# Twelve transposes of an identity between the first two score groups, and one key turn moved ahead of the second maxima

## Chip, cores and metric

The kernel runs on one core of a Trainium2 chip. The metric is the device time of one execution in microseconds (us); the figure for a kernel is the median of its runs. Everything is float32.

## The reference, cut to what matters

```
# q, k, v: (8 batches, 8 heads, 576 positions, 64); tau = 0.02
scores = q @ k^T / 8
thresh = max(scores, last axis) - tau
scores = where(scores >= thresh, scores, -1e9)
attn   = softmax(scores)
x      = (attn @ v), heads side by side: 4608 tokens x 512
h = x @ w_in        # 512 x 2048
g = relu(h) ** 2
out = g @ w_out     # 2048 x 512
```

## The kernel before, in words

**Visits and steps.** Attention is done in visits. A visit is one pair of heads of one batch; within a visit the 576 query rows are taken in blocks of 128, with a rest of 64. One block of one visit is a step, numbered s. The first four visits take only their blocks 0 and 1 (steps 0 to 7), so that the first tokens are complete early; later visits take what is left. Step 0 and step 1 are the two blocks of the first visit (number 0), steps 2 and 3 those of the second visit (number 1).

**What a step does, and on which engine.**

- `scores(s)` (line 273): TensorE multiplies 128 queries by the 576 keys, for two heads (u = 0 and 1) and two halves of the keys. That is four products, eight instructions, into two pairs of PSUM banks. Every step uses the first two pairs, banks 0 to 3, except step 1, which uses the list `second`, banks 4 to 7.
- `maxima(s, ...)` (line 310), called at the end of `scores`: VectorE takes the row maxima, one reduction for each head.
- `exponents` (lines 322, 323, 325): ScalarE makes the bias and the threshold from the maxima, and then two exponentials.
- `threshold` (lines 337, 339, 340): VectorE zeroes what is under the threshold, one instruction for each head. These are the last reads of the score banks, so that the next `scores` into the same banks waits for them.
- `divide` (lines 345, 347): GpSimd scales the weights.
- `turn` (lines 386, 387): TensorE transposes the weights by products with an identity, in three parts of three transposes; ScalarE copies each part out of PSUM. In the program of step s the first two parts belong to step s - 2 and stand between `scores(s)` and `exponents` of step s, both on TensorE's queue and on ScalarE's.
- `mix` (line 502): TensorE multiplies turned weights by values, three steps after the scores.

**Keys and queries of a visit.** `load_qk(n)` fetches the rows of visit n, and `prep(n)` turns them with one VectorE instruction each: `prep_part(q, n)` into `qT`, of which there is one buffer, and `prep_part(k, n)` into `kT[n % 2]`, of which there are two (both line 247). `qT` is read by the scores of both steps of a visit, so the queries of visit 1 can be turned only after `scores(1)` has read `qT`. The keys of visit 1 go into the other buffer.

**Start of the program.** After `load_qk(0)`, `load_qk(1)`, `load_v(0)` and the first three weight loads, VectorE does `prep(0)` and scales `ntau8` (line 1005). TensorE does `keep_busy(20)` (line 317): twenty transposes of the identity into bank 7 (`second[1][:, 1, ...]`), whose results nobody reads. Then the loop over s starts.

**What sets the order.** The kernel is scheduled by hand: the order of calls in the program is the order on each engine's queue, and engines wait for each other only by semaphores. In step 0 the loop calls `scores(0)`, `exponents` of step 0, and then, in the block `if s == 0` that the change touches, `scores(1)` and `prep(1)`; then `threshold` of step 0. Step 1 skips its own `scores` for that reason. From step 2 on, GpSimd, VectorE and ScalarE also round the feed-forward weights piece by piece (lines 149 to 158), and SyncE's queue loads keys, queries, values and weights in the order of the program.

From about a twentieth of the span on, the products of the feed-forward part (lines 548, 659, 730, 765) fill TensorE's queue between the score groups.

Of the kernel before, what the change touches and what calls it, by code (L numbers as in the profile page):

```python
# [19 lines left out]
def kernel(  # L20
# [117 lines left out]
    def round_weights(i, stage):  # L138

        words = weight_area(i).bitcast(U32).rearrange("p (n w) -> p n w", w=2)
        lo, hi = words[:, :, 0], words[:, :, 1]
        t, e, d = (turned[:, (i % 3 * 3 + x) * WP:(i % 3 * 3 + x + 1) * WP] for x in range(3))
        tu, eu = t.bitcast(U32), e.bitcast(U32)
        if stage == 0:
            nc.scalar.activation(out=e, in_=hi.bitcast(FP32), func=AF.Prelu, scale=2.0 ** -112, alpha=-2.0 ** 32)
            nc.scalar.activation(out=d, in_=lo, func=AF.Copy, scale=2.0 ** -52)  # L150
        elif stage == 1:
            nc.vector.tensor_scalar(out=tu, in0=eu, scalar1=3, scalar2=None, op0=ALU.logical_shift_left)
        elif stage == 2:
            nc.vector.tensor_scalar(out=eu, in0=tu, scalar1=0xFF800000, scalar2=None, op0=ALU.bitwise_and)
        elif stage == 3:
            nc.gpsimd.tensor_tensor(out=d, in0=d, in1=e, op=ALU.mult)
        else:
            nc.gpsimd.tensor_tensor(out=weight_piece(i)[1], in0=t.rearrange("p (h d) -> p h d", h=2),
                                    in1=d.rearrange("p (h d) -> p h d", h=2), op=ALU.add)

    def rows_of(n):
        return rows_in[n % 2 if n <= 2 * HP else 0]
# [8 lines left out]
    def load_qk(n):  # L171


        for x, t in ((rows_of(n)[1], k), (rows_of(n)[0], q)):
            for m in range(4):
                src, to = rows_32(t, n, m), x[m * 32:(m + 1) * 32, :, :]
                queue = nc.scalar if n == 0 and m % 2 else nc.sync
                last = REST // 32 if t is k and m >= 2 and not by_dma(n) else 0
                queue.dma_start(out=to[:, last:, :], in_=src[:, 0:S // 32 - last, :])
                if last:  # L180
                    queue = nc.gpsimd if n == 0 else nc.sync
                    queue.dma_start(out=to[:, 0:last, :], in_=src[:, S // 32 - last:, :])
# [20 lines left out]
    def arrived(t):  # L203
        assert all(x[0].tensor.name != t.tensor.name for x in loads)
# [27 lines left out]
    def prep(n):  # L232

        prep_part(q, n)
        prep_part(k, n)
# [8 lines left out]
    def prep_part(t, n):  # L244
        to, rows = (qT, rows_of(n)[0]) if t is q else (kT[n % 2], rows_of(n)[1])
        arrived(rows)
        nc.vector.transpose(to, rows.rearrange("p c d -> p (c d)"))
# [10 lines left out]
    def scores(s):  # L258


        vis, i = steps[s]
        n = 2 if i < NBLK else 1
        sc = [(second if s == 1 else pairs)[u] for u in range(n)]
        if i == NBLK:
            for half in range(2):
                nc.tensor.matmul(sc[0][:, half, 0:HALF], qmid, kT[vis % 2][:, half * HALF:(half + 1) * HALF], start=True, stop=True)  # L266
        else:
            halves = [(half, u) for half in range(2) for u in range(n)]
            if early():
                halves.sort(key=lambda x: x[1])  # L270
            for half, u in halves:
                rows = slice(u * D, (u + 1) * D)
                nc.tensor.matmul(sc[u][:, half, 0:HALF], qT[rows, i * P:(i + 1) * P],  # L273
                                 kT[vis % 2][rows, half * HALF:(half + 1) * HALF], start=True, stop=True)
        maxima(s, [x[:, :, 0:HALF] for x in sc])
# [28 lines left out]
    def maxima(s, sc):  # L304
        vis, i = steps[s]
        n = len(sc)
        st = stats[s % len(stats)]
        mx = st[:, 0, 0:n]
        for u in range(n):
            nc.vector.tensor_reduce(out=mx[:, u:u + 1], in_=sc[u], axis=AX.XY, op=ALU.max)  # L310
        w = w_slots[(s - first_dma) % (2 if by_dma(vis) else 3)][:, 0:n, :]
        weights[vis, i] = w, sc, st

    def keep_busy(times):

        for x in range(times):
            nc.tensor.transpose(second[1][:, 1, x % 4 * P:x % 4 * P + P], ident, ident)
# [301 lines left out]
    def some_later(engine):  # L619
        if later[engine]:  # L620
            make(*later[engine].popleft())
# [204 lines left out]
    def by_dma(n):  # L826

        return n >= 3 * HP - 1
# [34 lines left out]
    def early():  # L863
        return state["step"] < min(chunk_at)
# [231 lines left out]
    for s in range(END + 1):  # L1096
        state["step"] = s
        if s >= first_late:
            assert 4 not in kept.values()
            late_step(s)  # L1100
            continue
        state["usable"] = rounded_by[-1]
        rounded_by.append(state["rounded"])
        on = s < NST
        now = []
        if on:
            n, i = steps[s]
            at = visits[n][1].index(i)
            last = at == len(visits[n][1]) - 1
            now = list(range(done, done + pieces[s]))  # L1110
            done += pieces[s]
            more = n + 1 < len(visits)
            short = n < 2 * HP
            if short and at == 0 and 0 < n + 1 < 2 * HP:
                load_qk(n + 2)
            elif not short and at == 1 and not by_dma(n):
                load_qk(n + 1)
            if now:
                round_weights(now[0], 0)
            if s != 1:  # L1120
                scores(s)
                after()
                some_later("gpsimd")
        old = steps[s - 2] if 2 <= s < NST + 2 and not by_dma(steps[s - 2][0]) else None
        at_once = now or old or early()
        lay = on and last and more and not by_dma(n) and s != 1
        if old:
            turn(*old, 0)
            turn(*old, 1)
        if on:  # L1130
            exponents(n, i)
            if s and by_dma(steps[s - 1][0]):
                turn_last(s)
            for p in now[1:]:
                round_weights(p, 0)
            if at == 1:
                split_left(n)
            if lay:
                prep(n + 1)
            elif now:  # L1140
                for p in now:
                    round_weights(p, 1)
        if s in mixes and not old:
            mix(*mixes[s])
            for j in chunk_at.get(s, ()):
                add_chunk(j)
        quarter = rate(s) / 4 if s < END else 1e9
        fill(quarter)
        if s in mixes and old:
            mix(*mixes[s])  # L1150
            for j in chunk_at.get(s, ()):
                add_chunk(j)
        if old:
            turn(*old, 2)
        state["free"] = s > first_dma
        if s == 0:
            scores(1)
            prep(1)
        smooth = s > first_dma + 2 and s not in mixes
        some_later("vector")  # L1160
        some_later("gpsimd")
        if smooth:
            after()
        if on:
            threshold(n, i)
            for fn in prep_at[s] + load_at[s]:
                fn()
            if lay and now:
                round_weights(now[0], 1)
            if now:  # L1170
                round_weights(now[0], 2)
                round_weights(now[0], 3)
            for p in now[1:]:
                assert not lay
                round_weights(p, 2)
                round_weights(p, 3)
            if not at_once:
                divide(n, i)
        if smooth:
            fill(quarter)  # L1180
            after()
            some_later("gpsimd")
        for what in place_at[s]:
            place_blocks(*what)
        some_loads()
        some_later("vector")
        if not smooth:
            some_later("gpsimd")
            fill(quarter)
        some_loads()  # L1190
        if on and at_once:
            divide(n, i)
        fill(quarter)
        some_loads()
        fill(quarter)
        some_loads()
        if on:
            for p in now:
                end_rounding(p)
            if at == 0 and 0 < n <= 2 * HP:  # L1200
                load_v(n)
            elif last and n >= 2 * HP and not by_dma(n):
                load_v(n + 1)
# [35 lines left out]
```

## Time and profile before

| | |
|---|---|
| median of 3 runs | 1334.75 us (1334.66 to 1335.83) |
| profiled execution, its own time | 1334.19 us |
| span of its instructions | 1332.4 us |
| mean granted TensorE clock | 0.995 |
| TensorE busy | 1297.2 us, 97% of the span |
| VectorE busy | 928.2 us, 70% |
| ScalarE busy | 585.2 us, 44% |
| GpSimd busy | 758.3 us, 57% |
| chain that ended last | TensorE 85%, VectorE 5%, ScalarE 4%, DMA 3% |

The profiled execution is 1.8 us longer than its span: what lies before the first and after the last instruction. Its own time is 0.56 us under the median of the runs. Times in the trace count from the start of the span. "PE" is TensorE's matmul, "PEld" its weight load, "DVE" VectorE, "ACT" ScalarE, "POOL" GpSimd, "SP" SyncE. The granted clock is the share of its full clock at which TensorE was allowed to run.

### The profile page before, as it was taken

How to read it: one execution, taken by the hardware profiler on the slowest of the kernel's cores; microseconds unless marked ns; L12 is line 12 of the kernel's file. 1: busy time of each engine (PE TensorE's matmuls, PEld its weight loads, DVE VectorE, ACT ScalarE, POOL GpSimd, SP SyncE). 2: the span in 40 equal slices, each digit the busy share in tenths (PEclk: the TensorE clock that was granted, in tenths of full speed). 3: DMA queues.
4: the chain of work that ended last, by engine and by line, in shares of the span. 5: the costliest groups of instructions: out<-in, count | busy, mean ns of one | idle time of the engine just before them, and what ended most of it. 6: DMA issues, size and time to landing. Idle time of an engine off the chain costs nothing.

```text
span 1332.4 us, 25133 instructions
## 1 busy us (share of the span) xinstructions
PE 1297.2 (97%) x9112; PEld 1078.2 (81%) x9112; DVE 928.2 (70%) x2026; ACT 585.2 (44%) x1357; POOL 758.3 (57%) x865
## 2 busy tenths in 40 slices
PE   7898999999999999999999999999999999999998
PEld 5676556878796979787888888888887888889997
DVE  6877776777787878777786777868687877732131
ACT  4776674235262535343434443444434343422321
POOL 4689875765655555364655554737274737354451
PEclk7999999999999999999999999999999999999999
DMA  8764531647767686867586685758677577430000
GB/s 159 160 152 117 144 91 36 160 93 183 167 177 170 169 195 165 200 141 200 123 186 147 172 192 138 189 108 205 138 181 169 150 180 164 141 91 1 17 17 16
DMA packets 330124, 186.68 MB, mean 140 GB/s; under 512 B 291440, under 2 KB 291472, under 8 KB 323600
## 3 DMA queue, kind: packets, MB, share of 16 engines
q1 hardware_dynamic: 317696, 116.87, 45.0%
q10 hardware_dynamic: 9504, 59.27, 11.2%
q0 software_dynamic: 2800, 8.93, 1.8%
q8 instruction: 72, 1.18, 0.4%
q14 instruction: 52, 0.43, 0.1%
HBM read 109.22 MB, written 68.42 MB: 133 GB/s over the span
## 4 chain that ended last, share of the span: by engine, by line
PE 85%; DVE 5%; ACT 4%; DMA 3%; POOL 2%; issue 1%; SPq 1%; ACTq 0%; DVEq 0%; POOLq 0%
PE big L659 28%; PE big L765 27%; PE big L502 10%; PE big L289 8%; PE big L548 3%; PE big L273 3%; PE big L730 2%; PE big L386 2%; DMA wT<-aside 2%; DVE st L310 1%; DVE w L337 1%; ACT w L325 1%; ACT wT L387 1%; DMA aside<-turned 1%; PE big L266 0%
## 5 line engine op out<-in xcount | busy, mean ns | idle before, releaser
L337 DVE SCALAR_TENSOR_TENSOR w<-big,st,w 128x576 f32<-128x576 f32 x269 | 207.2, 807 | 97.8 <-ACT w L325 97.5
L310 DVE TENSOR_REDUCE st<-big 128x1 f32<-128x576 f32 x288 | 204.3, 748 | 86.2 <-PE big L289 53.5
L347 POOL TENSOR_SCALAR w<-w,st 128x576 f32<-128x576 f32 x269 | 247.4, 929 | 28.0 <-DVE st L340 24.0
L765 PE MATMUL big<-wo,gsum 128*128 128x256 f32 x1088 | 243.8, 382 | 0.0
L345 POOL TENSOR_SCALAR st<-st 128x2 f32<-128x2 f32 (+1 forms) x148 | 36.6, 247 | 358.6 <-DVE w L337 354.2
L765 PEld LDWEIGHTS big<-wo,gsum 128*128 128x128 f32 x1088 | 204.4, 190 | 37.1 <-issue 8.6
L659 PE MATMUL big<-xT,w_in_sb 128*128 128x128 f32 x1536 | 187.3, 277 | 0.8 <-DVE g L671 0.7
L659 PEld LDWEIGHTS big<-xT,w_in_sb 128*128 128x128 f32 x1536 | 178.5, 192 | 9.8 <-issue 7.6
L765 PE MATMUL big<-wo,g 128*128 128x256 f32 x816 | 185.3, 382 | 0.1
L325 ACT ACTIVATE w<-big,st 128x576 f32<-128x576 f32 x269 | 183.8, 734 | 0.2 <-ACT st L323 0.2
L502 PE MATMUL big<-wT,vs 128*64 128x128 f32 (+5 forms) x1700 | 164.8, 355 | 9.7 <-ACT wT L387 4.2
L765 PEld LDWEIGHTS big<-wo,g 128*128 128x128 f32 x816 | 151.6, 190 | 26.1 <-issue 6.5
L502 PEld LDWEIGHTS big<-wT,vs 128*64 128x64 f32 (+1 forms) x1700 | 97.3, 137 | 73.9 <-issue 21.5
L322 ACT ACTIVATE st<-st 128x2 f32<-128x2 f32 (+1 forms) x148 | 30.3, 205 | 263.4 <-DVE st L310 262.2
L671 DVE TENSOR_TENSOR g<-big,g 128x512 f32<-128x512 f32 x96 | 64.8, 677 | 82.3 <-PE big L659 76.4
L289 PE MATMUL big<-kT,qT 64*128 64x320 f32 (+3 forms) x768 | 108.0, 416 | 0.2 <-DVE w L337 0.2
L289 PEld LDWEIGHTS big<-kT,qT 64*128 64x128 f32 x768 | 84.5, 186 | 15.7 <-issue 4.3
L538 POOL TENSOR_TENSOR gsum<-g 128x512 f32<-128x512 f32 x34 | 46.1, 1356 | 81.6 <-ACT g L668 72.1
L667 ACT ACTIVATE g<-g 128x512 f32<-128x512 f32 x96 | 60.3, 628 | 61.0 <-DVE g L671 59.4
L668 ACT ACTIVATE g<-g 128x512 f32<-128x512 f32 x128 | 80.7, 630 | 4.1
L431 DVE STREAM_TRANSPOSE turned<-w 128x512 f32<-128x512 f32 x100 | 70.3, 703 | 3.7 <-DMA aside<-turned 2.6
L437 DVE STREAM_TRANSPOSE turned<-w 128x512 f32<-128x512 f32 x100 | 66.9, 669 | 0.0
(113 smaller groups left out, 1973.2 us busy)
## 6 DMA issues: line engine op xcount, KB each, us to landing
aside<-turned ACTq DMA_DIRECT2D x50, 1152.0 KB, 5.2
wT<-aside SPq DMA_DIRECT2D x200, 288.0 KB, 5.5
vs<-in_v_dram SPq DMA_DIRECT2D x72, 128.0 KB, 4.4
ql<-in_q_dram SPq DMA_DIRECT2D x126, 72.0 KB, 2.9
wo<-in_moe_w_in_dram SPq DMA_DIRECT2D x16, 512.0 KB, 4.8
wo<-in_moe_w_out_dram SPq DMA_DIRECT2D x16, 512.0 KB, 3.7
out_dram<-osb POOLq DMA_DIRECT2D x32, 256.0 KB, 3.3
kl<-in_k_dram SPq DMA_DIRECT2D x113, 72.0 KB, 3.0
```

Source lines behind the costliest of these rows:

```text
L289: nc.tensor.matmul(big[to, at + x0:at + x1], lhsT, keys[u * D:(u + 1) * D, x0:x1], start=True, stop=True)
L310: nc.vector.tensor_reduce(out=mx[:, u:u + 1], in_=sc[u], axis=AX.XY, op=ALU.max)
L325: nc.scalar.activation(out=w[:, u, :].rearrange("p (h k) -> p h k", h=2), in_=sc[u], func=AF.Exp, bias=bias[:, u:u + 1], scale=SCALE)
L337: nc.vector.scalar_tensor_tensor(out=wu, in0=sc[u], scalar=thr[:, u:u + 1], in1=wu, op0=ALU.is_ge, op1=ALU.mult, accum_out=sm[:, u:u + 1])
L347: nc.gpsimd.tensor_scalar(out=w[:, u, :], in0=w[:, u, :], scalar1=z[:, u:u + 1], scalar2=rcp[:, u:u + 1], op0=ALU.add, op1=ALU.mult)
L431: move(wb[:, 0:h, :, :], whole_[:, 0, :, :, :])
L437: move(wb[:, h + 1:, :, :], whole_[:, 1, :, :, :])
L502: nc.tensor.matmul(ps[u * D:(u + 1) * D, :], vs[n % 2][rows, u * (NBLK + 1) + c, :], wT[rows, at // REST:(at + ps.shape[1]) // REST, NBLK ...
L659: nc.tensor.matmul(to[:, f, :], factor(j, p, q, c)[:, f * P:(f + 1) * P], part[:, c, :], start=(p in "125" and f == 0 and c == 0), stop=(p ...
L668: nc.scalar.activation(out=to, in_=to, func=AF.Square)
L671: nc.vector.tensor_tensor(out=x, in0=to, in1=x, op=ALU.add)
L765: nc.tensor.matmul(to, left[:, f, :], wo[:, slot, f, :], start=(f == 0), stop=(f == HF - 1))
```

## The change

In step 0, the keys of visit 1 are turned before the scores of step 1 are issued, twelve transposes of the identity are put ahead of those scores, and only the queries of visit 1 are turned after them.

```diff
         if s == 0:
+            prep_part(k, 1)
+            keep_busy(12)
             scores(1)
-            prep(1)
+            prep_part(q, 1)
```

`prep(1)` was `prep_part(q, 1)` followed by `prep_part(k, 1)`. So on TensorE's queue the order becomes: eight instructions of `scores(0)`, twelve transposes of the identity (line 317), eight instructions of `scores(1)`. On VectorE's queue it becomes: two maxima of step 0, turn of the keys of visit 1, two maxima of step 1, turn of the queries of visit 1, `threshold` of step 0. The queues of ScalarE, GpSimd and SyncE keep their instructions and their order. `keep_busy` itself is unchanged:

```
    def keep_busy(times):
        for x in range(times):
            nc.tensor.transpose(second[1][:, 1, x % 4 * P:x % 4 * P + P], ident, ident)
```

## Prediction

> **What bounds the kernel now.** I first read the page's strip of slices, then the start of the trace, since the change lies at 9 to 14 us. TensorE is busy for 97% of the span and its clock is full everywhere but in the first slice:
>
> ```profile
> PE   7898999999999999999999999999999999999998
> PEclk7999999999999999999999999999999999999999
> ```
>
> The table of stretches (stretch, its length, then busy us and instruction count of PE, PEld, DVE, ACT and POOL, granted clock, DMA) places the loss:
>
> ```profile
> 8.06:11.48 3.42, 2.31 (x16) 1.68 (x16) 2.13 (x5) 0.25 (x2) 0.00 (x0) 1.00 0.72 129
> 11.48:14.89 3.41, 0.25 (x1) 0.25 (x2) 3.41 (x7) 2.94 (x7) 0.00 (x0) 1.00 0.78 198
> 14.89:18.30 3.41, 3.41 (x12) 2.23 (x12) 3.13 (x12) 1.24 (x2) 2.38 (x5) 0.50 1.08 350
> 18.30:21.71 3.41, 1.70 (x8) 1.30 (x8) 2.17 (x6) 2.88 (x7) 1.59 (x2) 0.50 0.87 129
> 113.88:117.29 3.41, 1.95 (x11) 1.39 (x10) 3.34 (x10) 2.47 (x8) 2.04 (x3) 1.00 0.55 166
> ```
>
> TensorE stands nearly idle from 11.48 to 14.89 us while VectorE is busy throughout, and then the clock is 0.50. In cuts of 0.2 us the clock is 0.73 in 14.8 to 15.0 and 0.64 in 28.4 to 28.6, so it falls at 14.89 and returns at 28.54. These 13.65 us at half clock are the whole loss: 13.65 x 0.5 / 1332.4 = 0.5%, and the mean clock is 0.995. What it costs is read from the timeline (start, us, instructions, last the idle time before and its releaser):
>
> ```profile
> 3.24 4.53 PE L317 MATMUL big<-ident 128*128 128x128 f32 x20 [3.24 <-POOL ident masks.py:199]
> 8.51 2.31 PE L273 MATMUL big<-kT,qT 64*128 64x288 f32 x16 [0.73 <-DVE ntau L1005]
> 9.78 2.75 DVE L310 TENSOR_REDUCE st<-big 128x1 f32<-128x576 f32 x4 [1.29 <-PE big L273]
> 14.64 3.02 PE L273 MATMUL big<-kT,qT 64*128 64x288 f32 x8 [3.82 <-DVE w L337]
> 17.59 2.18 PE L386 MATMUL big<-ident,w 128*128 128x128 f32 x9
> 20.60 0.82 DVE L337 SCALAR_TENSOR_TENSOR w<-big,st,w 128x576 f32<-128x576 f32 x1 [1.25 <-ACT w L325]
> 21.48 3.02 PE L273 MATMUL big<-kT,qT 64*128 64x288 f32 x8 [1.71 <-DVE w L337]
> 32.66 0.82 DVE L337 SCALAR_TENSOR_TENSOR wo<-big,st,wo 128x576 f32<-128x576 f32 x1 [0.79 <-ACT wo L325]
> 33.55 1.97 PE L273 MATMUL big<-kT,qT 64*128 64x288 f32 x8 [0.70 <-DVE wo L337]
> 37.86 0.82 DVE L337 SCALAR_TENSOR_TENSOR w<-big,st,w 128x576 f32<-128x576 f32 x1 [0.20 <-ACT w L325]
> ```
>
> A score group takes 3.02 us at half clock and 1.97 us at full. The first `threshold` instructions of steps 2, 3, 4 and 5 start at 20.60, 27.46, 32.66 and 37.86 us: two steps in the cold took 12.06 us, one warm step takes 5.20. The chain of waits says what a warm step is: scores 1.97, three transposes 0.49, two ScalarE copies 0.86, bias, threshold and exponential about 1.0, first `threshold` 0.84, next scores. So at half clock TensorE is on the path; at full clock much less of it is.
>
> **What the Trainium skill says.** Two parts of "TensorE: Matmul & The Clock Gate" bear on this. *Part 1: The HAM clock gate*: the clock is full or half, decided by a free-running window of 3413 ns; an idle window takes it down, a busy one brings it up. The trace agrees on the size: 28.54 - 14.89 = 13.65 us is four windows, and one back from 14.89 lies 11.48, the nearly idle stretch above. How much work keeps a window from counting as idle, neither the page nor this trace says: 0.25 us of 3.41 did not keep the clock up, 1.95 us (the 113.88 row) and 2.31 us (the 8.06 row) did. *Part 4: PE-mode transpose* says that transposes don't count as busy for this clock. Here the trace differs: the twenty transposes at the start step by about 0.22 us, as the nine cold ones at 17.59 do (4.53 / 20 = 0.23, 2.18 / 9 = 0.24), and right behind them sixteen score instructions take 2.31 us, where the cold rate would be 2 x 3.02. So these transposes did bring the clock up, by 8.06 us.
>
> **The change part by part.**
>
> *Twelve transposes.* They run at full clock. Warm ones: six took 0.87 us (30.25 us), three 0.55 us (32.30 us), so one is (0.87 - 0.55) / 3 = 0.107 us and a change of kind costs some 0.2 to 0.3 us once (0.87 - 6 x 0.107 = 0.23). The sum is 12 x 0.107 + 0.28 = 1.56 us. `scores(1)` ended at 10.82; it now ends at about 12.38.
>
> *Key turn moved ahead.* No instruction is added; one of 0.74 us (0.66 to the next) changes place. Its rows were loaded from 3.79 us on, the last key load of that visit issued by 6.84, and landings of this kind take 2.1 to 3.0 us, 6.1 at most, so the data is there by 11.1 at about 9 to 10. No DMA, on SyncE's queue or others, changes place. Maxima of step 0 keep 9.78 to 11.16; the key turn fills 11.12 to 11.85. VectorE could then start the maxima of step 1 at 11.77, but TensorE has them at 12.38 and one hop, 12.40: **a new wait of 0.63 us** (0.2 to 0.8 with the uncertain change of kind). Behind it on VectorE stand the query turn, which waits for `scores(1)` too, and `threshold` of step 0, for which `scores(2)` waits. Sum: `threshold` 13.79 to 14.42, `scores(2)` 14.64 to 15.27. The exponentials of step 1 move from 12.78 to 13.85 and end near 15.5, ahead of the rounding at 15.63 that waits for a weight load anyway, and ahead of their `threshold` (15.70 + 0.63). That is free, with 0.1 us to spare.
>
> *The clock.* TensorE's gap shrinks from 3.82 to 15.27 - 12.38 = 2.9 us. More to the point, the window 11.48 to 14.89 now holds 0.9 us of scores, not 0.25. The next two hold about 1.9 us (`scores(2)` at 15.27, 1.97 us) and 1.3 us (nine transposes, 0.107 each plus 0.23). I take it that none of the three counts as idle.
>
> *Step 2, warm.* Little is won here, because VectorE is the bound: `threshold` of step 1 now ends at 17.71 + 0.63 = 18.34, the two maxima of step 2 (17.62 + 0.63 = 18.25 on) end at 19.65, and only then can the bias of step 2 go. Before, it went at 19.55, held by a ScalarE copy behind cold transposes. Those transposes wait for `divide` of step 0 (GpSimd, 17.59 + 0.63 = 18.22); warm, the copies stand at 18.93 and 19.31, so the bias goes at 19.70. Step 2 ends 0.15 us late, `threshold` at 20.75. Cheaper scores are given back to VectorE and GpSimd.
>
> *Steps 3 and 4, warm.* Two steps cost 2 x 5.20 = 10.40 instead of 12.06: a gain of 1.66 us. `threshold` of step 4 comes at 31.15 instead of 32.66.
>
> *Sum.* 0.15 - 1.66 = **-1.5 us** on the path. From there on the order is fixed and engines wait only for each other, so I carry the shift to the end undiminished. The profiled execution would go from 1334.19 to 1332.7; since it stands 0.56 us under the median of the runs, I put the gain on the median: 1334.75 - 1.5 = 1333.2 us. Bounds for this case: if the change of kind costs nothing, 0.3 us less delay and up to -2.1; if VectorE's wait is 0.8 and stays in the path for one step, -0.9.
>
> **The rivals.**
>
> *The clock falls all the same at 14.89.* For it: 0.9 us in a window is less than any window shows that held the clock; scores use 64 of 128 rows, and two windows full of cold scores (14.89 and 21.71) did not bring the clock up. Against it: the only window that took the clock down was nearly empty. Then the 0.63 us wait is pure loss, since cold TensorE carries it through step 2: 1334.75 + 0.63 = 1335.4. If the clock's return also slips one window, because the transposes and mix that filled 25.13 to 28.54 start 0.63 later, step 4 is cold too: one more cold step, 6.86 - 5.20 = 1.7 us, 1337.1. **This is the slower side**; it decides where 0.9 us of work in 3.41 is not enough.
>
> *The clock falls one or two windows later*, at 18.30 or 21.71. Step 3 runs cold as before and step 2 has gained nothing: +0.15 to 0, 1334.8.
>
> *The gain is larger.* If the wait on VectorE does not appear, step 2 starts its bias about 0.4 us earlier, and with warm steps the gain is 2.1 us; with some queue further on that also gains from the shift, 2.7 or more, 1332.0. For it speaks that later stages pass through many short waits; nothing in the profile shows such a place.
>
> *The change doesn't do what it says*: if the moved turn made VectorE wait for keys. The landing times leave 1 us or more, so I give it nothing of its own.
>
> **How the numbers follow.** A measurement of this kernel can tell about 0.2%, 2.7 us, from no change: 1332.1 to 1337.4. Clock held, -1.5 us: 0.60. Clock falls at 14.89: 0.22, of which a third near 1337. Falls later: 0.08. Larger gain: 0.10. From the first case a tenth may pass -2.7 by a carry over 1, so faster is 0.10 + 0.04 = 0.14; slower takes a third of the second case, where the end of the range is crossed: 0.08; the rest, 0.78, is within. The likeliest time is 1333.2 us. The range takes in the first case, the later fall and the milder form of the second: 1331.9 to 1336.2.
>
> **What the profile after would show.** Right: clock 1.00 in all stretches up to 40 us, mean clock 1.000; VectorE waiting some 0.6 us for L273 before the third maxima; `scores(2)` near 15.3; score groups of at most 2 us from there; first `threshold` instructions at about 20.75, 25.95 and 31.15. Wrong: half clock from 14.89 on, or `threshold` of step 4 no earlier than 32.66; or that one early and the end not, which would fault the carry.

## The result and the profile after

The changed kernel takes 1339.23 us, median of 8 runs (1337.63 to 1341.34), against 1334.70 us for 8 runs of the kernel before (1333.41 to 1336.67). The ratio is 1.0033, 95% interval 1.0022 to 1.0043: slower by about 4.5 us, where 1.5 us less was forecast. The profiled execution took 1338.87 us, span 1337.1 us, 4.7 us over that of before.

The strips of the page (busy tenths and granted clock in 40 slices) look as before, but for one digit in each: the clock of the first slice, and TensorE's busy share of the fifth:

```profile
PE   7898899999999999999999999999999999999998
PEclk8999999999999999999999999999999999999999
```

The timeline of the start (start, us, instructions, idle time before and its releaser):

```profile
8.80 1.25 PE L273 MATMUL big<-kT,qT 64*128 64x288 f32 x8 [1.29 <-DVE ntau L1005]
9.98 1.53 PE L317 MATMUL big<-ident 128*128 128x128 f32 x12
11.41 0.77 DVE L247 STREAM_TRANSPOSE kT<-wo 128x576 f32<-128x576 f32 x1
11.44 1.25 PE L273 MATMUL big<-kT,qT 64*128 64x288 f32 x8
12.71 1.42 DVE L310 TENSOR_REDUCE st<-big 128x1 f32<-128x576 f32 x2 [0.53 <-PE big L273]
15.58 2.04 PE L273 MATMUL big<-kT,qT 64*128 64x288 f32 x8 [2.90 <-DVE w L337]
21.05 0.82 DVE L337 SCALAR_TENSOR_TENSOR w<-big,st,w 128x576 f32<-128x576 f32 x1 [0.22 <-ACT w L325]
21.93 3.02 PE L273 MATMUL big<-kT,qT 64*128 64x288 f32 x8 [1.97 <-DVE w L337]
33.11 0.82 DVE L337 SCALAR_TENSOR_TENSOR wo<-big,st,wo 128x576 f32<-128x576 f32 x1 [1.14 <-ACT wo L325]
```

Here the first queries landed 0.3 us later than in the profile of before (7.31 against 7.01 us), so times are best taken from `scores(0)`. The twelve transposes take 1.53 us, VectorE waits 0.53 us for the second scores, `scores(2)` runs at full clock, and `scores(3)` at half again. The table of stretches, cut where this execution's clock changed (stretch, length, busy us and instructions of PE, PEld, DVE, ACT, POOL, clock, DMA):

```profile
10.54:13.95 3.41, 2.14 (x17) 1.44 (x15) 2.88 (x5) 1.65 (x4) 0.00 (x0) 1.00 0.69 137
13.95:17.36 3.41, 1.78 (x8) 1.30 (x8) 3.27 (x9) 2.88 (x6) 0.68 (x2) 1.00 0.97 370
17.36:20.78 3.42, 2.44 (x10) 1.69 (x9) 3.28 (x9) 1.74 (x5) 3.01 (x5) 0.50 1.07 170
266.54:269.95 3.41, 1.96 (x11) 0.99 (x12) 2.94 (x9) 1.92 (x6) 0.51 (x2) 1.00 0.14 25
566.91:570.32 3.41, 1.36 (x13) 0.75 (x11) 1.72 (x5) 1.60 (x4) 3.17 (x4) 1.00 1.19 151
570.32:573.74 3.42, 3.42 (x19) 1.45 (x16) 2.90 (x6) 0.14 (x1) 2.42 (x4) 0.50 0.40 60
```

The clock fell at 17.36 us instead of 14.89, behind a stretch with 1.78 us of TensorE work in it. It fell for one stretch more at 269.95 and again at 570.32, where the kernel before kept it. But the first steps are not where the time went: `threshold` of step 4 is at 33.11 against 32.66, 0.45 us late, and the end is 4.7 us late. The rest is lost in a few places hundreds of microseconds on. Around 260 us the queries of a later visit are turned (VectorE's timeline, before and then after):

```profile
255.80 0.73 DVE L247 STREAM_TRANSPOSE kT<-kl 128x576 f32<-128x576 f32 x1
261.34 0.78 DVE L247 STREAM_TRANSPOSE qT<-ql 128x576 f32<-128x576 f32 x1 [4.81 <-DMA ql<-in_q_dram]
```

```profile
256.30 0.73 DVE L247 STREAM_TRANSPOSE kT<-kl 128x576 f32<-128x576 f32 x1
263.75 0.78 DVE L247 STREAM_TRANSPOSE qT<-ql 128x576 f32<-128x576 f32 x1 [6.71 <-DMA ql<-in_q_dram]
```

The key turn is 0.50 us late, the query turn 2.41. The query turn waits for two loads, issued 0.35 us apart. The first landed after 2.0 us in both kernels; the second took 4.4 us instead of 2.5, and that is the difference. The view of these loads has, before and then after:

```profile
DMA to landing us min/median/max: 2.0/2.2/2.5
```

```profile
DMA to landing us min/median/max: 2.0/3.2/4.4
```

Some of this is covered; 1.5 us are left by 287 us. TensorE's timeline at two later places, after:

```profile
569.42 4.10 PE L502 MATMUL big<-wT,vs 128*64 128x256 f32 x24 [2.05 <-DMA wT<-aside]
573.46 3.84 PE L765 MATMUL big<-wo,gsum 128*128 128x256 f32 x16
...
1179.07 2.37 PE L502 MATMUL big<-wT,vs 128*64 128x320 f32 x16
1182.79 2.63 PE L502 MATMUL big<-wT,vs 128*64 128x256 f32 x24 [1.34 <-DMA wT<-aside]
1185.35 3.84 PE L659 MATMUL big<-xT,w_in_sb 128*128 128x128 f32 x32
```

and before:

```profile
567.57 2.63 PE L502 MATMUL big<-wT,vs 128*64 128x256 f32 x24 [1.36 <-DMA wT<-aside]
570.14 3.72 PE L765 MATMUL big<-wo,gsum 128*128 128x256 f32 x16
...
1175.67 5.08 PE L502 MATMUL big<-wT,vs 128*64 128x320 f32 x40
1180.68 3.84 PE L659 MATMUL big<-xT,w_in_sb 128*128 128x128 f32 x32
```

Near 570 us the wait for turned weights is 0.69 us longer, the clock falls behind it, and 24 instructions take 4.10 us instead of 2.63: between line 502 starting (1.85 us late) and line 765 starting (3.32 us late) 1.5 us are lost. Near 1180 us a wait of 1.34 us appears inside a run of 40 products that had none.

So the question for the runs was: what do twelve transposes at 10 us have to do with loads at 260 and 1180 us?

### The profile page after: what moved, and what is told of

It is laid out like the page before. It is cut to its first block, busy times and chain, and to the rows that moved or that the text cites. A ratio compares the mean times of both kernels' runs of the same rounds, so it can differ in the third digit from the quotient of the medians.

```text
span 1337.1 us, 25159 instructions
## 1 busy us (share of the span) xinstructions
PE 1299.7 (97%) x9124; PEld 1079.2 (81%) x9124; DVE 926.0 (69%) x2026; ACT 584.9 (44%) x1357; POOL 756.4 (57%) x865
## 3 DMA queue, kind: packets, MB, share of 16 engines
q8 instruction: 72, 1.18, 0.4%
## 4 chain that ended last, share of the span: by engine, by line
PE 83%; DVE 5%; DMA 4%; ACT 3%; POOL 3%; issue 1%; SPq 0%; ACTq 0%; DVEq 0%; POOLq 0%
PE big L659 29%; PE big L765 27%; PE big L502 10%; PE big L289 8%; PE big L273 3%; PE big L730 2%; PE big L548 2%; DMA wT<-aside 1%; PE big L386 1%; DMA aside<-turned 1%; DVE w L337 1%; DVE st L310 1%; ACT w L325 1%; ACT wT L387 1%; POOL w L347 1%
```

## The experiments

Theory A: the early delay of VectorE grows later. Theory B: the 24 added TensorE instructions (twelve transposes with their weight loads) cost something later, whatever they delay. Theory C: the moved key turn changes what the loads do. Each kernel was timed in rounds beside the kernel before, and the ratios are to that; its median in these rounds was 1335.25 to 1336.12 us. Each kernel has one profile, so a figure from a trace is that of one execution.

**Only the turn moved.**

```diff
-            scores(1)
-            prep(1)
+            prep_part(k, 1)
+            scores(1)
+            prep_part(q, 1)
```

> Only the key turn of visit 1 is moved ahead of scores(1); no transposes are added. VectorE then has the same instructions in another order, so threshold of step 0 starts within 0.1 us of before, and TensorE's program is unchanged. Theory A (the early delay of VectorE, 0.63 us in the changed kernel, is what grows later): within 1 us of before, about 1334.7. Theory B (the 24 added TensorE instructions, whatever they delay): also about 1334.7. Theory C (the moved turn changes what the loads do later): +3 us or more, 1338 to 1339.

Measured: 1334.93 us, ratio 0.9996 (0.9988 to 1.0005). Theory C falls.

**Only the transposes.**

```diff
+            keep_busy(12)
             scores(1)
             prep(1)
```

> Only the twelve transposes are added ahead of scores(1); both turns of visit 1 stay behind the second maxima. VectorE then idles about 1.3 us before the second maxima (11.2 to 12.4), so threshold of step 0 starts 1.3 us late instead of 0.63. Theory A: at least the +4.5 us of the changed kernel, 1339 to 1341, and more of it in later waits than in the changed kernel. Theory B: +4.5 us, 1339 to 1340. Theory C: +1 to 1.5 us, about 1336.

Measured: 1339.77 us, ratio 1.0037 (1.0025 to 1.0050). `threshold` of step 4 was 1.75 us late (34.41), so that about 3 us came later. The total fits A and B alike; A had also expected more of it in later waits than in the changed kernel, and there is not more. Part of the early delay is the clock: the first eight score instructions took 2.30 us here against 1.25 in the changed kernel, though both start alike.

**The transposes where they delay nothing.**

```diff
             scores(1)
+            for x in range(12):
+                nc.tensor.transpose(second[1][:, 1, HALF:HALF + P], ident, ident)
             prep(1)
```

> The twelve transposes stand behind scores(1), into columns of bank 7 that no score uses, in TensorE's gap before scores(2); the turns stay as before. TensorE's program has the same 24 added instructions, but nothing on VectorE is delayed. Theory A: no loss, 1334.7, or a gain of up to 1.7 us to 1333.0 if the gap no longer takes the clock down. Theory B: +4.5 us all the same, 1339. Theory C: 1334.7.

Measured: 1338.63 us, ratio 1.0024 (1.0015 to 1.0034), although `threshold` of step 4 came at 32.27, 0.39 us earlier than before. Theory A falls, and B is left. The profile also shows why filling this one gap does not hold the clock; stretches as above:

```profile
13.07:16.48 3.41, 2.88 (x19) 2.21 (x17) 3.27 (x9) 2.07 (x5) 0.64 (x2) 1.00 0.97 323
16.48:19.90 3.42, 1.79 (x10) 0.97 (x9) 2.84 (x9) 2.44 (x7) 3.24 (x5) 1.00 0.97 205
```

At 19.90 us it fell all the same, behind 1.79 us of work in 3.42: step 2 has a second gap, from the nine transposes to `scores(3)`.

**The delay without the transposes.**

```diff
-            scores(1)
-            prep(1)
+            prep_part(k, 1)
+            prep_part(k, 1)
+            scores(1)
+            prep_part(q, 1)
```

> The keys of visit 1 are turned twice ahead of scores(1), and no transposes are added: one more VectorE instruction of 0.66 us, so threshold of step 0 starts 0.66 us late, as in the changed kernel, while TensorE's program is that of before. Theory A: +4 us, about 1339. Theory B: +0.5 us, about 1335.2. Theory C: like the changed kernel less its transposes, +3 us or more.

Measured: 1335.36 us, ratio 1.0005 (0.9996 to 1.0014), with `threshold` of step 4 at 33.64, 0.98 us late. The delay costs what it is, or less.

**What the program length does.** The Trainium skill, "Runtime: NRT & Kernel Launch", section *Instruction fetch mechanics*, says that an engine's program is streamed in blocks of 16 KiB, 256 instructions, through a DMA queue of the sequencer's own, and that the cost is mostly hidden. The traces agree on the block: the page's list of DMA queues has `q8 instruction: 72, 1.18`, 72 packets and 1.18 MB, 16.4 KB each. The cost that is not hidden here, as the next runs show, is one to other transfers. With 24 instructions more ahead, every later block begins 24 instructions earlier in the work and so can be fetched beside other transfers. B1 is this theory; B2 says that the work of the transposes in the gap is what counts.

**The changed kernel at equal length, first try.**

```diff
+    def wide(times):
+        for x in range(times):
+            nc.tensor.matmul(second[1][:, 1, :].rearrange("p (a n) -> p a n", n=P), ident,
+                             ident.unsqueeze(1).to_broadcast([P, 4, P]), start=True, stop=True)
-    keep_busy(20)
+    wide(5)
+    keep_busy(2)
...
+            prep_part(k, 1)
+            wide(2)
+            keep_busy(4)
             scores(1)
-            prep(1)
+            prep_part(q, 1)
```

> The changed kernel with as many TensorE instructions as before: the twenty transposes at the start become five wide products of the identity (four instructions each with their weight loads, the same 4.3 us) and two transposes, and the twelve in the middle become two wide products and four transposes of the same 1.28 us. The early delay of VectorE and the order of the turns are those of the changed kernel. Theory B1 (the number of TensorE instructions ahead of the rest counts, because the 16 KB blocks in which its program is fetched then begin at other places): the +4 us goes, 1334.5 to 1335.5. Theory B2 (the work of the transposes in that gap counts): 1338.5 to 1339.5 as in the changed kernel.

Measured: 1337.58 us, ratio 1.0016 (1.0008 to 1.0023), between the kernel before and the changed one, and not what was expected. The wide products took twice the time planned: `scores(0)` began at 10.18 us and `threshold` of step 4 at 35.87, 3.2 us late. The end, 2.1 us late, holds no more than that, but the run is confounded and was made again, below.

**24 instructions more, at the start.**

```diff
-    keep_busy(20)
+    for x in range(24):
+        nc.tensor.transpose(second[0][0:D, 0, x % 4 * P:x % 4 * P + D], ident[0:D, 0:D], ident[0:D, 0:D])
+    keep_busy(8)
```

> The kernel before, with 24 TensorE instructions more and no more work: at the start 24 transposes of a 64x64 identity and eight of 128x128 take the place of the twenty of 128x128, about the same 4.3 us, all ahead of the data. Nothing after the start is changed. Theory B1: +3 to +4.5 us, 1338 to 1339, with the losses near 260, 560 and 1180 us that the changed kernel has. Theory B2: within 0.5 us of before.

Measured: 1339.97 us, ratio 1.0028 (1.0017 to 1.0040). `threshold` of step 4 was 1.93 us late (34.59): the first sixteen score instructions took 4.16 us instead of 2.31, so the clock came up late. Whether the smaller transposes are the reason is not shown, since the run with only the transposes also began cold behind the twenty of before. Some 1.9 of the 3.7 us are the start in this profile, and the rest came later.

**20 instructions less.**

```diff
-    keep_busy(20)
+    wide(5)
```

> The kernel before, with 20 TensorE instructions less and the same 4.3 us of work at the start: five wide products of the identity for twenty transposes. Theory B1: the blocks begin elsewhere again, so a shift of either sign of 1 us or more is likely, and the waits near 260, 560 and 1180 us differ from those of before; the loss need not be that of 24 more. Theory B2: within 0.5 us of before.

Measured: 1337.61 us, ratio 1.0012 (1.0004 to 1.0020). `threshold` of step 4 was 0.34 us late (33.00); the other 1.3 us came later. A shorter program is no better in itself.

**Equal length, transposes behind the scores, first try.**

```diff
-    keep_busy(20)
+    wide(5)
+    keep_busy(2)
...
             scores(1)
+            for x in range(8):
+                nc.tensor.transpose(second[1][:, 1, HALF:HALF + P], ident, ident)
             prep(1)
```

> As many TensorE instructions as before: the start as in the run with the changed kernel at equal length, and eight transposes behind scores(1), in columns that no score uses, where they delay nothing on VectorE; both turns stay behind the second maxima. Theory B1: none of the +4 us; a gain of up to 1 us for what is saved of the half clock, 1333.8 to 1334.8. Theory B2: 1337.5 to 1339.

Measured: 1335.82 us, ratio 1.0001 (0.9991 to 1.0011). Its scores, too, began 1.0 us late, and `threshold` of step 4 was at 32.45, 0.21 us early. Against the 1338.63 us of the run with the transposes in the same place and a longer program, 2.3 points in a thousand are gone (with eight transposes behind the scores here and twelve there).

**The changed kernel at equal length, mended.**

```diff
-    keep_busy(20)
+    wide(2)
+    keep_busy(4)
...
+            prep_part(k, 1)
+            keep_busy(12)
             scores(1)
-            prep(1)
+            prep_part(q, 1)
```

> The changed kernel, its twelve transposes and both turns where it has them, with the start made shorter by 24 TensorE instructions: two wide products of the identity (1.7 us each at half clock) and four transposes for the twenty transposes. TensorE's program is then as long as before from the twelve transposes on, and the start takes its old 4.3 us; in the earlier run at equal length the wide products took twice what was planned, and the scores began 1.7 us late. Theory B1 (place of the program blocks): 1.0 us or less over before, of which 0.6 us is VectorE's wait; no loss of over 1 us near 260 and 1180 us. Theory B2 (the work in the gap): +4 us as in the changed kernel.

Measured: 1335.68 us against 1335.61, ratio 1.0000 (0.9989 to 1.0010). The change as it stands, with its transposes, its wait on VectorE and its turns, costs nothing measurable when TensorE's program keeps its length. B2 falls. One part of B1's forecast failed: the profile has a wait of 1.63 us near 1180 us.

**24 instructions more and nothing else.**

```diff
+    for x in range(12):
+        nc.tensor.transpose(second[0][0:32, 0, 0:32], ident[0:32, 0:32], ident[0:32, 0:32])
     keep_busy(20)
```

> The kernel before with twelve transposes of a 32x32 identity ahead of the twenty at the start, 24 TensorE instructions and about 0.6 us that end before the data is there. Scores of step 0 start as before, at 8.5 to 8.8 us. Theory B1: +3 to +4.5 us, with waits for queries near 260 us and for values near 1180 us that before does not have. Theory B2: within 0.5 us of before.

Measured: 1338.14 us, ratio 1.0018 (1.0010 to 1.0025): +2.4 us (1.3 to 3.3), well over B2's 0.5 us, and less than the 3 to 4.5 us that B1 expected. `scores(0)` began at 8.60 and `threshold` of step 4 at 32.79, 0.13 us late.

**A candidate.** The start of the mended run, and twelve transposes behind `scores(1)`:

```diff
-    keep_busy(20)
+    wide(2)
+    keep_busy(4)
...
             scores(1)
+            for x in range(12):
+                nc.tensor.transpose(second[1][:, 1, HALF:HALF + P], ident, ident)
             prep(1)
```

> A candidate for a faster kernel: TensorE's program as long as before (start of two wide products and four transposes), and twelve transposes behind scores(1), where they delay nothing on VectorE; the turns stay behind the second maxima. The clock should fall about one step later than before or not at all. Threshold of step 4 comes 0.4 to 1.5 us earlier than before. Theory B1: a gain of 0.4 to 1.5 us at the end. Theory B2: +3 us. A third theory, that later stages give back what the first 60 us gain: no change.

Measured: 1334.78 us, ratio 0.9996 (0.9987 to 1.0005). The clock fell at 20.3 us, `threshold` of step 4 came at 32.05, 0.61 us early (0.12 of it because the scores began so much earlier), and no gain can be told at the end. The early time itself is not surely gained: in the next run, whose start is that of the kernel before, `threshold` of step 4 came at 31.81 us, because the clock there fell at 12.95 us and was up again at 19.78. TensorE's timeline has the step that is still cold:

```profile
14.53 1.97 PE L273 MATMUL big<-kT,qT 64*128 64x288 f32 x8 [0.53 <-DVE w L337]
16.73 1.57 PE L386 MATMUL big<-ident,w 128*128 128x128 f32 x9 [0.23 <-POOL w L347]
20.88 3.02 PE L273 MATMUL big<-kT,qT 64*128 64x288 f32 x8 [2.58 <-DVE w L337]
```

**24 instructions more, late.**

```diff
             late_step(s)
+            if s == 110:
+                for x in range(12):
+                    nc.tensor.transpose(big[0:32, 2464:2496], ident[0:32, 0:32], ident[0:32, 0:32])
             continue
```

> The kernel before with the same twelve transposes of a 32x32 identity put in late, in the program of step 110 (some 800 us into the span), 24 TensorE instructions and about 0.4 us of work. Theory B1: nothing of the losses near 260 and 560 us, since the blocks before that point begin where they did; the loss near 1180 us (1.3 us) is there, so +1 to +2 us in all. Theory B2, or a cost of any longer program wherever the instructions stand: +3.5 us, or +0.4 us if only work counts.

Measured: 1337.13 us, ratio 1.0012 (1.0005 to 1.0018). They ran at 848.6 us. The query wait near 260 us is that of before (4.97 us), and the wait near 1180 us is there, as B1 says. Two things were not expected: the insertion cost 0.8 us (0.52 us of work behind a wait of 0.30 us for VectorE), and this profile also lost 2.5 us near 570 us, ahead of the insertion. So the loss near 570 us does not need moved blocks.

**One block more, and one block and 24 instructions more.** The loop of the small transposes at the start with 128 and with 140 passes:

```diff
+    for x in range(128):
+        nc.tensor.transpose(second[0][0:32, 0, 0:32], ident[0:32, 0:32], ident[0:32, 0:32])
     keep_busy(20)
```

> The kernel before with 128 transposes of a 32x32 identity ahead of the twenty at the start: 256 TensorE instructions more, which is one 16 KB block at 64 bytes each. They delay the scores of step 0 by some 4 to 7 us, since twelve of them took 0.6 us before and only 0.7 us of room is there. If the place of the blocks counts (B1), every later block begins at the same work as before: the delay of the first 20 us is carried to the end, nothing is added near 260 and 1180 us, and the query load near 260 us lands without a program block beside it. If each added instruction costs something later, the loss is far over that of 24.

> The same with 140 small transposes, 280 instructions: one block and 24 instructions, so that the blocks begin where they begin in the changed kernel. The start is delayed 0.3 to 0.6 us more than with 128. B1: 2.5 to 5 us slower than with 128, with the waits near 260 and 1180 us back. If the number alone counts, or nothing but the delay: 0.3 to 0.8 us slower than with 128.

Measured: 1342.10 us with 128, ratio 1.0056 (1.0043 to 1.0070), and 1344.92 us with 140, ratio 1.0076 (1.0063 to 1.0088). `threshold` of step 4 was 5.18 us late with 128 and 5.83 with 140. So 0.65 us of the 2.8 between them is the start, and about 2.1 us come from 24 instructions on top of 256. With 128, the interval, 5.7 to 9.3 us, still lies 0.5 to 4.2 us over the start's delay, and no run here says where that is lost; its profiled execution shows nothing added near 260 or 1180 us, but took 1338.52 us, the fastest of the five, 3.6 us under their median. VectorE's timeline, with 128 and then with 140:

```profile
266.83 0.78 DVE L247 STREAM_TRANSPOSE qT<-ql 128x576 f32<-128x576 f32 x1 [5.10 <-DMA ql<-in_q_dram]
```

```profile
269.25 0.78 DVE L247 STREAM_TRANSPOSE qT<-ql 128x576 f32<-128x576 f32 x1 [6.83 <-DMA ql<-in_q_dram]
```

**All profiles together.** For each run: how long VectorE had waited when the query turn near 260 us began; whether a program block of TensorE (queue q8) was fetched in the 5 us before it; the median time from issue to landing of the query loads in that time; the wait in the products near 1180 us.

| kernel | TensorE instructions ahead of 260 us, against before | query wait, us | block beside it | query load, us | wait near 1180 us, us |
|---|---|---|---|---|---|
| before | 0 | 4.81 | no | 2.2 | 0 |
| turn only | 0 | 4.86 | no | 2.2 | 0 |
| turned twice | 0 | 5.11 | no | 2.4 | 0 |
| equal length, first try | 0 | 5.02 | no | 2.3 | 0 |
| equal length behind, first try | 0 | 5.30 | no | 2.5 | 0 |
| equal length, mended | 0 | 5.13 | no | 2.4 | 1.63 |
| candidate | 0 | 4.95 | no | 2.4 | 0 |
| 24 more, late | 0 | 4.97 | no | 2.3 | 1.02 |
| 128 small | +256 | 5.10 | no | 2.4 | 0 |
| 20 less | -20 | 4.96 | no | 2.3 | 0.56 |
| changed kernel | +24 | 6.71 | yes | 3.2 | 1.34 |
| transposes only | +24 | 6.49 | yes | 3.1 | 1.30 |
| transposes behind | +24 | 6.24 | yes | 2.9 | 1.47 |
| 24 more at the start | +24 | 6.43 | yes | 3.0 | 1.49 |
| 24 small at the start | +24 | 6.29 | yes | 2.9 | 1.28 |
| 140 small | +280 | 6.83 | yes | 3.2 | 1.27 |

The DMA view of the changed kernel from 256 to 264 us, the time of the two query loads, has the block (queue and kind with packets, MB, share), and that of before has no such row:

```profile
q8 instruction: 1, 0.02, 0.7%
```

Near 260 us the two groups don't overlap: 4.8 to 5.3 us without a block, 6.2 to 6.8 with one. The median of the two loads hides how much one of them lost: the second took 3.9 to 4.5 us with a block beside it and 2.5 to 3.0 without.

The other two places have a block as well, but beside a store. The turned weights that TensorE waits for there are first stored to memory from ScalarE's queue (line 408, `aside<-turned`) and then loaded by SyncE (line 449), and the loads wait until the store has landed. Before and changed kernel:

| store near | kernel | issued, us | block fetched, us after the issue | store landed, us after the issue |
|---|---|---|---|---|
| 570 us | before | 554.69 | 4.2 | 4.9 |
| 570 us | changed | 555.35 | 1.0 | 6.1 |
| 1180 us | before | 1163.89 | 5.6 | 6.4 |
| 1180 us | changed | 1167.29 | 2.7 | 7.6 |

Over all profiles, near 1180 us the store took 7.3 to 7.8 us in the seven kernels whose block came 2.3 to 3.0 us after the issue, and 6.3 to 6.4 in eight of the nine whose block came 5.3 us after it or later; the ninth is the mended kernel, with 7.9 us, though its block came at 5.8 us as in the others. In the kernel with 20 instructions less, the block came late enough (1177.14 us) to stand beside the loads instead, and the last of these took 7.0 us, against 6.2 to 6.4 in the other fifteen. Near 570 us it took 5.8 to 6.2 us in the five whose block came within 1.0 us after the issue, and 4.8 to 5.4 in the ten whose block came 3.9 to 4.4 us after it. In the sixteenth (24 more at the start) the block came 0.8 us ahead of the issue, and the store took 4.2 us.

## Why the prediction was wrong

**Right, by its own steps.** The transposes were put at 1.56 us and took 1.53. The key turn found its data, and moving it cost nothing (ratio 0.9996); had the last key load taken the 6.1 us that the prediction names as the most, counted from 6.84, it would have come too late at 12.9. `scores(2)` was to come 0.63 us late: counted from `scores(0)` it came 0.65 late (6.78 us against 6.13). Step 2 was to end 0.15 us late because VectorE and GpSimd bound it: counted so, its `threshold` was 0.16 late (12.25 against 12.09). Its nine transposes were cold (2.18 us), not warm as assumed, but the bias of step 2 waited last for VectorE's maxima, as forecast.

**The step on the clock failed.** "I take it that none of the three counts as idle" was wrong for the stretch with `scores(2)`: 1.78 us of TensorE work in 3.41 did not hold the clock, and it fell at 17.36. The prediction also took the edges of the stretches from the profile of before, and they lie elsewhere in each execution: with TensorE's program unchanged the clock fell at 13.68 us (turn only) and 15.05 (turned twice), and in the changed kernel an edge lay at 13.95. `scores(3)` was cold (3.02 us), and the gain of 1.66 us on steps 3 and 4 did not come: `threshold` of step 4 was 0.16 us late, counted from `scores(0)`, not 1.5 early. That is the rival of the later fall, 1334.8 us. The mended run, which has the change at the old program length, measured what that rival says: no difference, within 1.5 us. The 1.66 us itself holds one cold step, 6.86 us against 5.20: the second of the "two steps in the cold" had taken 5.20 us already. Two small sums are off and change nothing: nine transposes at 0.107 us and 0.23 make 1.2 us, not 1.3, and a tenth of 0.60 is 0.06, not 0.04.

**The carry to the end failed, and it set the sign.** The sum counted what twelve transposes do in their place and then carried the shift to the end "undiminished", because "the order is fixed and engines wait only for each other". The order is; the loads are not only the program's own. TensorE's instructions are loaded too, and 24 more of them move the fetch of each later block. 24 small transposes in an otherwise idle start cost +2.4 us by themselves; 256 more instructions leave the wait near 260 us as it was, and 24 on top of those bring it back; the changed kernel at its old program length loses nothing that can be measured. The longer program is therefore shown to be the cause of most of the 4.5 us: 3.3 points in a thousand with it, 0.0 (-1.1 to 1.0) without. That it acts through the place of the blocks, and not through their number, is shown near 260 us by the pair of 256 and 280; for the time at the end the pair speaks for it (2.1 us), with five runs each and the open remainder with 256.

**What is only argued, and what stays open.** That a block delays the query load because both go through the same DMA engines is inferred from their meeting: in all six profiles that have the longer wait near 260 us and in none of the other ten, and beside the slower stores at the two later places. Near 260 us that is about 1 us at the end of the step; near 1180 us, 1.3 us, though the mended kernel has such a wait with its block where the kernels without it have theirs. The loss near 570 us (a store that took 1.2 us longer, a wait 0.7 us longer, and the clock falling behind it) also came once without moved blocks, so how much of it they cause is open. Why the changed kernel lost more (4.5 us) than 24 small transposes (2.4 us, interval 1.3 to 3.3) is not settled either: 0.5 us of the difference is the early delay. Their profiled executions have the same span, 1337.1 us, and the kernel before measured 1334.70 us beside the one and 1335.61 beside the other, so the rest may lie in the intervals.

**The rivals.** The slower one, a fall at 14.89 and a slip of the clock's return, gave 1335.4 to 1337.1 and did not happen. The larger gain did not either. None named a cost far from the place of the change.

## What to carry to other kernels

Count the instructions that an edit adds to an engine's program, not only their time: on this long unrolled program with tight loads, 24 instructions at the start moved a block fetch beside a load that VectorE waited for, 250 us later, and that load landed 1.9 us later. To tell such a shift from the edit's own effect, run the edit once at equal program length, and once its length without its work. And price a clock that is to be held by the gaps that remain: with one gap of two filled, the clock still fell, at 17.15 to 23.5 us, and nothing was gained that could be measured.

## What the runs showed of the hardware

- No busy time of TensorE in a stretch of 3.41 us decided alone whether the clock fell. In the changed kernel it fell behind 1.36 us (566.91 to 570.32), 1.78 us (13.95 to 17.36) and 1.96 us (266.54 to 269.95); it held behind 1.49 us in the first-try kernel of equal length with the transposes behind the scores (the line below), and behind 1.95 us in the kernel before (113.88). The prediction took 0.9 and 1.3 us as enough.

```profile
566.22:569.63 3.41, 1.49 (x14) 0.92 (x12) 1.72 (x5) 1.62 (x4) 3.18 (x4) 1.00 1.20 147
569.63:573.05 3.42, 3.42 (x26) 2.27 (x22) 2.90 (x6) 0.76 (x3) 3.10 (x5) 1.00 0.35 54
```

- One 16.4 KB block of TensorE's program, fetched within 5 us of a query load, went with 2.9 to 3.2 us from issue to landing instead of 2.2 to 2.5 (median of two loads; 3.9 to 4.5 us instead of 2.5 to 3.0 for the second).
- 256 added instructions made one packet more on q8 (73, 1.20 MB) and left the wait near 260 us at 5.10 us; 280 made it 6.83.
